# A scheduling planner inside a kernel: new instruction costs, a new price for accumulating DMAs, and two requests moved to other stages

## Chip, cores and metric

The kernel runs on one core of one Trainium2 chip. The metric is the device time of one execution in microseconds (us), inputs and outputs in the chip's memory.

## The reference

Three blocks follow each other. The tensor that passes between them has 2304 rows (4 batches of 576 positions) of 512 columns.

- Attention with a bias: 4 x 8 heads, 576 positions, head size 64, causal, with scores lowered by running sums of a third input.
- A first expert block with one expert: `h = x @ w_in` (512 to 2048), `g = h * sigmoid(1.702 h)`, `g @ w_out`.
- A second expert block with eight experts, all of them used for every row:

```python
logits = x @ w_gate
P = exp(logits - logits.max())
for _ in range(8):                 # rows, then columns, are normalised
    P /= P.sum(1, keepdims=True) + 1e-09
    P /= P.sum(0, keepdims=True) + 1e-09
    P *= N / E
for e in range(8):                 # w1: 512 x 1024, w2: 1024 x 512
    h = np.maximum(x @ w1[e], 0.0)
    out += P[:, e:e + 1] * (h @ w2[e])
```

## The kernel before, in words

The program is written out by Python into five instruction queues (PE, ACT, DVE, POOL, and SP for DMAs), and each queue runs strictly in its written order. A recording layer, the class `Sequencer`, decides that order while the program is built. Every operation on ACT, DVE, POOL and SP is first held back; PE's are issued at once, in the order that the planner takes them. The planner keeps a clock for each engine: `cost` (L127) says how long an operation keeps its engine, `depend` (L187) when a result can be used by another operation (the end of the first plus an entry of `LATENCY`), `issue` (L194) moves the clocks on. `run` lets each engine take, among its held operations that are ready by its clock, the one of lowest `rank`. PE's next step is chosen from the step that is ready first by the same clocks. So all waits are real, but which instruction stands ahead of which on a queue rests on the planner's estimates.

For a DMA the planner keeps one common clock, `dma`: each transfer adds its bytes at 360 bytes per nanosecond and ends 440 ns later, plus `late`, a supplement (2000 ns for background work in the second block). A DMA of background rank is held back while that clock is more than `BACKLOG` (3000 ns) ahead.

`fine` is switched on where the second expert block is prepared (L1824); there other cost formulas hold. For `fine`, a DVE operation keeps its engine 150 ns plus its elements at 0.96 or 1.92 per ns, an ACT operation 165 ns (input in PSUM) or 200 ns plus its elements at 1.2 per ns, with 190 ns more where it also writes a sum.

The second block takes the tokens in three groups `tp` of 768. Both matrix products use a seven-product scheme (Strassen's) on half-size blocks, each number as a pair of f16 parts. For each expert `e` and group `tp` there are four units `unit1` (`x @ w1`; seven products of 6 matmuls of 384 columns) and three units `unit2` (`h @ w2`; seven products M1 to M7 of 12 matmuls of 256 columns). Two units are in flight, each on four PSUM banks A to D. A product is added onto the bank of an earlier one: bank B begins as an ACT copy of A (`B<-A`), C as an ACT copy of B (`C<-B`), and the matmuls that add to a copied bank must wait for the copy. Results of `unit2` are scaled into tiles `y` (4 buffers) by ACT or DVE. For the first expert `y` is written to memory, for the second it is joined with that, and for experts 2 to 6 it is added to `acc_d` in memory by an accumulating DMA from POOL's queue (`leave`), 18 for each expert, 90 in all.

While expert `e` runs, the weights of `e + 1` are prepared in the background, at rank 2: `weight_scales` (L1232) loads all of w1 and w2 in 16 pieces of 256 KB (tiles `wm`, in a ring of 7 buffers that it shares with the loads `wr`) and squares each on ACT to find the largest value; `prep_w1` and `prep_w2` (L1423, L1461) load the weights again (`wr`), form the seven combinations and split them into f16 parts, `w1o` in place and `wo` by way of memory (`w2_d`); `load_w2` (L1483) fetches the latter (`w2o`). `load_x2` fetches a token group (`xt`). `after1` (L2096) and `after2` (L2113) are called when a unit is over, and ask for these. What is asked for then waits in the queues above until the planner finds room.

## Time and profile before

| | |
|---|---|
| median of 3 runs | 2025.22 us |
| the runs | 2023.23 to 2025.8 us |
| span of the profiled execution, first to last instruction | 2019.1 us |
| PE / DVE / ACT / POOL busy | 97% / 69% / 62% / 17% of the span |
| first matmul of the second expert block | near 656 us |
| last matmul | 2013.2 us |

The profile is of one execution; of its own time the page gives the span alone. The median of the runs is 6.1 us longer than that span: what lies around the span, and the spread of the runs. "Idle before" an instruction is how long its engine stood still ahead of it, and the arrow names what ended that. A row of the timeline can stand for several equal instructions that follow each other (x12).

### The profile page before, as it was taken

What the parts mean: (1) busy time and instruction counts of PE and PEld (TensorE: products, weight loads), DVE (VectorE), ACT (ScalarE), POOL (GpSimd) and SP (SyncE); (2) the same over time, 40 slices, a digit from 0 to 9 for tenths busy, and PEclk for the clock granted to TensorE, in tenths of its full rate; (3) what the DMA queues carried; (4) which work ended last, traced back from release to release, by engine and by line L of the source; (5) the groups of instructions that cost most, each with busy time, mean ns of one, the idle gap of its engine ahead of it and who ended that gap; (6) DMA issues with size and microseconds to landing.
All of it is one profiled execution on the core that took longest, in us unless ns stands there. A gap on an engine that the chain in (4) does not pass through costs nothing.

```text
span 2019.1 us, 41044 instructions
## 1 busy us (share of the span) xinstructions
PE 1961.6 (97%) x15683; PEld 1575.5 (78%) x15683; DVE 1398.8 (69%) x3036; ACT 1258.0 (62%) x2571; POOL 335.4 (17%) x376
## 2 busy tenths in 40 slices
PE   6989999999999999999999999999998999999998
PEld 5889999999988777777777777777776777777776
DVE  5886777776643677868857866775775787577555
ACT  4776766766534676666666765756665676566444
POOL 3564444453200000000010100111110000111000
PEclk9999999999999999999999999999999999999999
DMA  7555444453354654566585676667657567666331
GB/s 219 157 175 189 134 134 133 141 145 106 85 139 137 184 171 160 184 199 211 174 216 160 160 228 125 172 175 168 187 148 197 133 177 202 120 187 170 118 129 53
DMA packets 234421, 323.18 MB, mean 160 GB/s; under 512 B 40800, under 2 KB 160288, under 8 KB 234224
## 3 DMA queue, kind: packets, MB, share of 16 engines
q1 hardware_dynamic: 221264, 296.96, 46.5%
q0 software_dynamic: 12960, 23.60, 9.2%
q8 instruction: 123, 2.02, 0.4%
q14 instruction: 74, 0.61, 0.1%
HBM read 231.90 MB, written 84.35 MB: 157 GB/s over the span
## 4 chain that ended last, share of the span: by engine, by line
PE 75%; DVE 9%; DMA 7%; issue 5%; ACT 4%; SPq 0%; POOL 0%; ACTq 0%; DVEq 0%; POOLq 0%
PE C L269 14%; PE D L269 14%; PE A L269 14%; PE hp L269 9%; PE B L269 8%; PE acc L269 5%; PE sp L269 3%; PE op L269 3%; PE tp L269 2%; DMA wm<-in_moe_w_dram 2%; DVE h L269 2%; PE accw L269 2%; DMA w_d<-wo 2%; ACT h L269 1%; DVE t L269 1%
## 5 line engine op out<-in xcount | busy, mean ns | idle before, releaser
L269 PEld LDWEIGHTS <-h 128*128 128x128 f16 x6048 | 592.2, 98 | 111.8 <-issue 32.1
L269 PEld LDWEIGHTS <-w1o 128*128 128x128 f16 x4036 | 394.8, 98 | 252.7 <-issue 1.9
L269 POOL DMA_DIRECT2D acc_d<-y x90 | 77.9, 866 | 1209.4 <-DVE y L269 1117.4
L269 PE MATMUL A<-w2o,h 128*128 128x256 f16 x1728 | 215.0, 273 | 16.0 <-ACT B L269 14.0
L269 PE MATMUL C<-xt,w1o 128*128 128x384 f16 x1152 | 218.6, 326 | 0.2
L269 PE MATMUL D<-xt,w1o 128*128 128x384 f16 x1152 | 216.4, 326 | 0.0
L269 PE MATMUL D<-w2o,h 128*128 128x256 f16 x1728 | 214.8, 273 | 0.3 <-ACT y L269 0.2
L269 PE MATMUL A<-xt,w1o 128*128 128x384 f16 x1152 | 215.0, 326 | 0.1
L269 PE MATMUL C<-w2o,h 128*128 128x256 f16 x1728 | 205.4, 272 | 7.8 <-ACT C L269 6.7
L269 DVE SCALAR_TENSOR_TENSOR h<-hst,h 128x768 f16<-128x768 f32 (+1 forms) x192 | 142.2, 752 | 48.4 <-ACT h L269 47.5
L269 PE MATMUL hp<-xh,wih 128*128 128x256 f32 (+1 forms) x512 | 153.9, 301 | 1.2 <-DVE stats L269 0.6
L269 PE MATMUL hp<-xl,wih 128*128 128x256 f32 (+1 forms) x512 | 151.5, 296 | 0.0
L269 PE MATMUL hp<-xh,wil 128*128 128x256 f32 (+1 forms) x512 | 151.4, 296 | 0.0
L269 ACT ACTIVATE h<-hst 128x768 f16<-128x768 f32 (+1 forms) x192 | 128.9, 678 | 6.1 <-DVE hst L269 6.0
L269 ACT COPY C<-B 128x384 f32<-128x384 f32 (+1 forms) x168 | 71.4, 425 | 85.1 <-PE B L269 68.6
L269 ACT ACTIVATE hst<-A 128x384 f32<-128x384 f32 x96 | 47.0, 490 | 119.2 <-PE A L269 118.5
L269 ACT ACTIVATE sm<-sm,stats 64x576 f32<-64x576 f32 (+4 forms) x160 | 94.6, 600 | 37.0 <-DVE stats L269 36.6
L269 PE MATMUL acc<-gh,woh 128*128 128x256 f32 x384 | 110.9, 289 | 0.0
L269 PE MATMUL B<-w2o,h 128*128 128x256 f16 x864 | 109.7, 275 | 0.0
L269 PE MATMUL B<-xt,w1o 128*128 128x384 f16 x576 | 109.3, 326 | 0.0
L269 PE MATMUL acc<-gl,woh 128*128 128x256 f32 x384 | 108.5, 282 | 0.0
L269 PE MATMUL acc<-gh,wol 128*128 128x256 f32 x384 | 108.4, 282 | 0.0
(235 smaller groups left out, 4041.9 us busy)
## 6 DMA issues: line engine op xcount, KB each, us to landing
xt<-xc_d SPq DMA_DIRECT2D x168, 384.0 KB
wm<-in_moe_w_dram SPq DMA_DIRECT2D x112, 256.0 KB
w2o<-w_d SPq DMA_DIRECT2D x56, 512.0 KB
wr<-in_moe_w_dram SPq DMA_DIRECT2D x112, 256.0 KB
w_d<-wo SPq DMA_DIRECT2D x98, 256.0 KB
acc_d<-y POOLq DMA_DIRECT2D x90, 256.0 KB, 6.0
kq<-in_qk_dram SPq DMA_DIRECT2D x32, 448.0 KB
st<-in_moe_w_in_dram SPq DMA_DIRECT2D x16, 512.0 KB
```

The source lines that it names most:

```text
L269: self.seq.submit(self.name, what, lambda: method(*args, **named), outs, ins)
```

## The change

Cost formulas of the planner, for the second block (`fine`): a DVE operation keeps its engine 66 ns (was 150) plus its elements, and 60 (was 63) for a scalar taken from a tile; an ACT operation 50 or 90 ns (was 165 or 200), 100 (was 95) for such a scalar and 93 (was 190) for a sum. What was taken off comes back as a `tail`: the result counts as written 85 (DVE) or 110 ns (ACT) after the engine is free, 90 more with a sum. A dependent operation on the same engine is ready 34 ns after that (it was the full latency between engines, 128 or 150).

DMAs: an accumulating DMA counts 3.6 times its bytes on the planner's DMA clock. The 16 loads of `weight_scales` count as landing 3000 ns later (`LATE`), for experts 2 and up.

Requests: `weight_scales(e + 1)` is asked for after the first unit1 of group 0 (was: after the fourth), `prep_w2(e + 1)` after the third unit2 of group 0 (was: after the fourth unit1 of group 1).

```diff
--- before.py
+++ after.py
@@ -37,8 +37,11 @@
 ASKED = 12
 BACKLOG = 3000
 N_KF = 4
+ADDING = 3.6
+AFTER_OWN = 34
 N_F = 14
 NEXT_V = 11
+LATE = 3000.0
 
 LATENCY = {
     "PE": 197, "ACT": 150, "DVE": 128, "POOL": 75,
@@ -47,7 +50,7 @@
 
 
 class Op:
-    __slots__ = ("engine", "call", "cost", "ready", "end", "waits", "after", "rank", "number", "nbytes", "late")
+    __slots__ = ("engine", "call", "cost", "ready", "end", "waits", "after", "rank", "number", "nbytes", "late", "tail")
 
 
 class Sequencer:
@@ -124,7 +127,7 @@
             n *= x
         return n
 
-    def cost(self, engine, what, out, ins):
+    def cost(self, engine, what, out, ins, sums=False):
         n = max(self.size(x) for x in [out] + ins[:2])
         psum = any(x.space == PSUM for x in ins)
         if self.fine:
@@ -133,9 +136,9 @@
             by = any(self.size(x) == 1 for x in ins[1:]) and n > 1
             if engine == "DVE":
                 quick = what in ("tensor_copy", "tensor_scalar") and not psum
-                return 150 + 63 * by + n / (1.92 if quick else 0.96)
+                return 66 + 60 * by + n / (1.92 if quick else 0.96)
             if engine == "ACT":
-                return (165 if psum else 200) + 95 * by + n / 1.2
+                return (50 if psum else 90) + 100 * by + 93 * sums + n / 1.2
         if engine == "PE":
             n = self.size(out)
             if what == "transpose":
@@ -150,17 +153,22 @@
         return 80 + n * {"memset": 0.3, "tensor_scalar": 2.7}.get(what, 2.24)
 
 
-    def submit(self, engine, what, call, outs, ins):
+    def submit(self, engine, what, call, outs, ins, adds=False):
         op = Op()
         op.engine, op.call, op.end, op.rank, op.number = engine, call, None, self.rank, self.count
-        op.ready, op.waits, op.after, op.nbytes = 0.0, set(), [], 0
+        op.ready, op.waits, op.after, op.nbytes, op.tail = 0.0, set(), [], 0, 0
         op.late = self.late + (2000 if self.fine and self.rank else 0)
         self.count += 1
         if what == "dma_start":
             op.cost = 60 if engine == "SP" else 1000
             op.nbytes = self.size(outs[0]) * outs[0].shape[0] * (2 if self.fine and outs[0].dtype == F16 else 4)
+            if adds and self.fine:
+                op.nbytes *= ADDING
         else:
-            op.cost = self.cost(engine, what, outs[0], ins) + (190 if len(outs) > 1 else 0)
+            sums = len(outs) > 1
+            op.cost = self.cost(engine, what, outs[0], ins, sums) + (190 if sums and not self.fine else 0)
+            if self.fine:
+                op.tail = {"DVE": 85, "ACT": 110}.get(engine, 0) + 90 * sums
         for ap, writes in [(x, False) for x in ins] + [(x, True) for x in outs]:
             name = ap.tensor.name
             if name in self.outside:
@@ -183,11 +191,12 @@
         else:
             self.held[engine].append(op)
 
-    @staticmethod
-    def depend(op, on):
+    def depend(self, op, on):
         if on.end is None:
             op.waits.add(on)
             on.after.append(op)
+        elif self.fine and on.engine == op.engine != "PE" and not on.nbytes:
+            op.ready = max(op.ready, on.end + AFTER_OWN)
         elif on.engine != "PE" or op.engine != "PE":
             op.ready = max(op.ready, on.end + LATENCY.get((on.engine, op.engine), LATENCY.get(on.engine, 0)))
 
@@ -197,7 +206,8 @@
                 self.issue(x)
         e = op.engine
         start = max(self.free[e], op.ready)
-        self.free[e] = op.end = start + op.cost
+        self.free[e] = start + op.cost
+        op.end = start + op.cost + op.tail
         if op.nbytes:
             self.issued = max(self.issued, start) + 475
             self.dma = max(self.dma, self.issued + 1200) + op.nbytes / 360
@@ -266,7 +276,7 @@
                 ins = ([lhs] if lhs is not None else []) + aps + list(keys.values())
             else:
                 ins = aps + list(keys.values())
-            self.seq.submit(self.name, what, lambda: method(*args, **named), outs, ins)
+            self.seq.submit(self.name, what, lambda: method(*args, **named), outs, ins, "accum_op" in named)
 
         return ask
 
@@ -1234,15 +1244,19 @@
         mx = mem["small"].tile([128, 2, 8], F32, tag="wmx", name="wmx", bufs=2)
         for i in range(8):
             st = raw([128, 2, 256], "wm")
+            seq.late = LATE if e > 1 else 0.0
             nc.sync.dma_start(
                 out=st, in_=w1[e, i // 4 * 256:i // 4 * 256 + 256, i % 4 * 256:i % 4 * 256 + 256]
                 .rearrange("(c p) f -> p c f", p=128)
             )
+            seq.late = 0.0
             squares(mx[:, 0, i:i + 1], st)
         scale_of(("w1", e), mx[:, 0], True)
         for i in range(8):
             st = raw([128, 1, DM], "wm")
+            seq.late = LATE if e > 1 else 0.0
             nc.sync.dma_start(out=st, in_=w2[e, i * 128:(i + 1) * 128, :].rearrange("p (o d) -> p o d", o=1))
+            seq.late = 0.0
             squares(mx[:, 1, i:i + 1], st)
         scale_of(("w2", e), mx[:, 1], True)
         iw = mem["small"].tile([128, 1], F32, name=f"iw{e}")
@@ -2096,14 +2110,12 @@
     def after1(e, tp, j):
         if j % 2 and tp == NTP - 1 and e + 1 < E:
             later(2, prep_w1, e + 1, j // 2)
+        if (tp, j) == (0, 0) and 0 < e < E - 1:
+            later(2, weight_scales, e + 1)
         if j < NJ - 1:
             return
         if (e, tp) != (E - 1, NTP - 1):
             later(1, load_x2, (tp + 1) % NTP)
-        if tp == 0 and 0 < e < E - 1:
-            later(2, weight_scales, e + 1)
-        if tp == 1 and 0 < e < E - 1:
-            later(2, prep_w2, e + 1)
 
     def after_gate(tp):
         if tp == NTP - 1:
@@ -2111,6 +2123,8 @@
             side.append((x, next(x)))
 
     def after2(e, tp, i):
+        if (tp, i) == (0, 2) and 0 < e < E - 1:
+            later(2, prep_w2, e + 1)
         if (tp, i) == (NTP - 1, 2) and e + 1 < E:
             later(1, load_w2, e + 1)
 
```

No instruction that computes is added or taken away; the queues are in another order. The number of rows on PE is the same (26536), and its first difference stands in the first unit of the second block. Three places, as the built programs have them:

ACT, expert 5, the time of the last unit2 pair of group 0. `wm` is a square of `weight_scales`, B and C are copies into banks, `y` results. Before:

```order
L269 COPY C_20551<-B_20444 128x256
L269 ACTIVATE wm,wmx<-wm 128x512 x2
L269 COPY C_20565<-B_20450 128x256
L269 ACTIVATE wm,wmx<-wm 128x512 x6
L269 ACTIVATE y<-C_20565,pq 128x256
L269 ACTIVATE wm,wmx<-wm 128x512
L269 COPY B_20649<-A_20636 128x256
L269 COPY B_20677<-A_20670 128x384
L269 ACTIVATE y<-D_20652,pq 128x256
L269 ACTIVATE y<-A_20636,pq 128x256
```

Now:

```order
L279 ACTIVATE wm,wmx<-wm 128x512
L279 COPY C_20597<-B_20440 128x256
L279 ACTIVATE wm,wmx<-wm 128x512
L279 COPY B_20613<-A_20600 128x256
L279 ACTIVATE wm,wmx<-wm 128x512 x6
L279 COPY C_20692<-B_20613 128x256
L279 ACTIVATE y<-B_20613,pq 128x256
L279 COPY B_20701<-A_20694 128x384
L279 ACTIVATE wm,wmx<-wm 128x512
L279 ACTIVATE m_20739<-D_20731 128x384
L279 ACTIVATE y<-A_20600,pq 128x256
L279 ACTIVATE y<-C_20692,pq 128x256
```

The six squares in one piece stood ahead of a `y` and a seventh square, and of the copy of A into B for the last unit2 of the group. Now the one square ahead of this copy is the ninth, the six come behind it, and the sixteenth square stands two copies later.

SP, the same expert, the loads between those of `w2o` and those of the second token group. `mx` is a column of maxima, written when eight squares are done. Before:

```order
L269 DMA wm<-in_moe_w_dram 128x2x256 x7
L269 DMA xt<-xc_d_206 128x1536 x7
L269 DMA wm<-in_moe_w_dram 128x2x256
L269 DMA wm<-in_moe_w_dram 128x512 x7
L269 DMA mx_20374<-m_20370 128x1
L269 DMA wm<-in_moe_w_dram 128x512
L269 DMA mx_20387<-m_20383 128x1
L269 DMA row<-mx_20374 128x128
```

Now:

```order
L279 DMA wm<-in_moe_w_dram 128x2x256 x8
L279 DMA xt<-xc_d_206 128x1536 x7
L279 DMA wm<-in_moe_w_dram 128x512 x3
L279 DMA mx_20139<-m_20135 128x1
L279 DMA wm<-in_moe_w_dram 128x512 x5
L279 DMA row<-mx_20139 128x128
L279 DMA mx_20152<-m_20148 128x1
L279 DMA wr<-in_moe_w_dram 128x2x256 x6
L279 DMA row<-mx_20152 128x128
```

The first `mx` now goes out after the eleventh load, behind it five loads; it went out after the fifteenth. One load more stands ahead of `xt`, and the first `wr` loads of `prep_w2` stand ahead of the last `row`.

PE, expert 4, group 2: the end of M6 of one unit2 in bank B and what follows. Before:

```order
L269 MATMUL C1_19863<-w2o_18065,h_19705 128x256
L269 LDWEIGHTS h_19705
L269 MATMUL B0_19771<-w2o_18065,h_19705 128x256
L269 LDWEIGHTS h_19705
L269 MATMUL B0_19771<-w2o_18065,h_19705 128x256
L269 LDWEIGHTS h_19705
L269 MATMUL B0_19771<-w2o_18065,h_19705 128x256
L269 LDWEIGHTS h_19472
L269 MATMUL C0_19898<-w2o_18065,h_19472 128x256
```

Now:

```order
L279 MATMUL B0_19749<-w2o_18066,h_19644 128x256
L279 LDWEIGHTS h_19710
L279 MATMUL B0_19749<-w2o_18066,h_19710 128x256
L279 LDWEIGHTS h_19710
L279 MATMUL B0_19749<-w2o_18066,h_19710 128x256
L279 LDWEIGHTS h_19710
L279 MATMUL B0_19749<-w2o_18066,h_19710 128x256
L279 LDWEIGHTS h_19470
L279 MATMUL C1_19871<-w2o_18066,h_19470 128x256
```

Before, M5 of the same unit, on bank C0, which is the copy of B0, followed at once. Now 12 matmuls of the other unit (C1) stand between M6 and M5.

## Rows read from the trace of the kernel before

**Rows 1.** The page, section 1: busy time, share and instructions of each engine.
```profile
PE 1961.6 (97%) x15683; PEld 1575.5 (78%) x15683; DVE 1398.8 (69%) x3036; ACT 1258.0 (62%) x2571; POOL 335.4 (17%) x376
```

**Rows 2.** Waits of PE over the span: waiting, awaited, total us, times, longest us.
```profile
PE A L269 <- ACT B L269: 14.0, 18, 5.1
...
PE C L269 <- ACT C L269: 6.7, 14, 1.0
```

**Rows 3.** Timeline of PE, second block: start us, us, instruction, [idle before it, releaser].
```profile
691.18 1.47 PE L269 MATMUL A<-w2o,h 128*128 128x256 f16 x12 [0.25 <-ACT B L269]
...
1048.05 1.47 PE L269 MATMUL A<-w2o,h 128*128 128x256 f16 x12 [0.99 <-ACT B L269]
...
1153.22 4.09 PE L269 MATMUL C<-w2o,h 128*128 128x256 f16 x36 [0.50 <-ACT C L269]
...
1216.83 1.47 PE L269 MATMUL A<-w2o,h 128*128 128x256 f16 x12 [0.84 <-ACT B L269]
...
1385.42 1.47 PE L269 MATMUL A<-w2o,h 128*128 128x256 f16 x12 [1.77 <-ACT B L269]
...
1729.28 0.92 PE L269 MATMUL A<-w2o,h 128*128 128x256 f16 x7 [1.70 <-ACT B L269]
...
1878.78 1.47 PE L269 MATMUL A<-w2o,h 128*128 128x256 f16 x12 [0.28 <-ACT B L269]
```

**Rows 4.** Timeline of PE after the longest stop, and in undisturbed work near the end.
```profile
1558.30 2.72 PE L269 MATMUL A<-w2o,h 128*128 128x256 f16 x12 [5.08 <-ACT B L269]
...
1560.81 2.77 PE L269 MATMUL B<-w2o,h 128*128 128x256 f16 x12
...
1563.37 1.56 PE L269 MATMUL D<-w2o,h 128*128 128x256 f16 x12
...
2006.05 1.47 PE L269 MATMUL A<-w2o,h 128*128 128x256 f16 x12
...
2007.36 1.47 PE L269 MATMUL D<-w2o,h 128*128 128x256 f16 x12
```

**Rows 5.** Timeline of ACT around the longest stop.
```profile
1546.65 0.61 ACT L269 ACTIVATE wm<-wm 128x512 f32<-128x512 f32 x1
...
1547.29 0.63 ACT L269 ACTIVATE wm<-wm 128x512 f32<-128x512 f32 x1
...
1554.33 0.63 ACT L269 ACTIVATE wm<-wm 128x512 f32<-128x512 f32 x1 [6.32 <-DMA wm<-in_moe_w_dram]
...
1557.26 0.63 ACT L269 ACTIVATE wm<-wm 128x512 f32<-128x512 f32 x1 [1.24 <-DMA wm<-in_moe_w_dram]
...
1557.88 0.74 ACT L269 COPY B<-A 128x256 f32<-128x256 f32 x2
```

**Rows 6.** Timelines of SP's queue and of POOL, the same time.
```profile
1531.24 3.21 SPq L269 DMA_DIRECT2D xt<-xc_d  x7
...
1539.56 0.33 SPq L269 DMA_DIRECT2D wm<-in_moe_w_dram  x1
1542.22 0.33 SPq L269 DMA_DIRECT2D wm<-in_moe_w_dram  x1
...
1545.72 0.38 SPq L269 DMA_DIRECT2D wm<-in_moe_w_dram  x1
...
1545.73 0.86 POOL L269 DMA_DIRECT2D acc_d<-y  x1 [37.99 <-DVE y L269]
```

**Rows 7.** Windows: stretch, busy PE, PEld, DVE, ACT, POOL (x instructions), PEclk, DMA share, GB/s.
```profile
1535.00:1540.00 5.00, 5.00 (x47) 4.48 (x47) 4.77 (x9) 4.87 (x12) 0.00 (x0) 1.00 0.99 362
1545.00:1550.00 5.00, 4.46 (x41) 4.01 (x41) 1.40 (x3) 3.01 (x11) 2.59 (x3) 1.00 1.08 105
...
1555.00:1560.00 5.00, 1.70 (x9) 1.20 (x9) 0.16 (x1) 2.79 (x9) 0.86 (x1) 0.67 1.01 171
```

**Rows 8.** The accumulating DMAs (tile acc_d): time to landing.
```profile
DMA to landing us min/median/max: 3.9/6.0/15.9
```

**Rows 9.** Groups: line, engine, operation, shapes, count | busy us, mean ns | idle before.
```profile
L269 PE MATMUL C<-xt,w1o 128*128 128x384 f16 x1152 | 218.6, 326 | 0.2
```

## The prediction

> **What bounds the kernel now.** I read the page first, then the waits of PE, then PE's timeline stop by stop, and beside the longest stop the timelines of ACT, SP and POOL. PE is busy for 1961.6 us, 97% of the span [rows 1], so only the time in which it stands still, or runs slowly, can be won; none of its matmuls goes. Then the waits of PE: what is long in the second block are waits for ACT's copies of one bank into another, 14.0 us in 18 stops for `B<-A`, 6.7 us in 14 for `C<-B`, 20.7 us together [rows 2]. PE's timeline, read in windows of 10 us from 650 us to the end, has each of them.
>
> Among the 18, five are long: 0.99, 0.84, 1.77 and 1.70 us [rows 3] and 5.08 us [rows 4], 10.38 us together, one in each of the experts 2 to 6, the five whose results are added by accumulating DMAs. The other 13 are of one kind, 0.25 to 0.28 us, 3.6 us together, the first at 691.18, the last at 1878.78 [rows 3]. Of the 14, five are 0.50 us, the first at 1153.22 [rows 3].
>
> The longest stop tells what the long ones are. ACT had six squares, the 10th to the 15th, in its queue ahead of the copy that PE wanted. The 13th began at 1547.29; then ACT stood still for 6.32 us, until the 14th load had landed, and again 1.24 us for the 16th; at 1557.88 came the copy [rows 5]. I measure from the moment when SP sends the first load of the next tokens, 1531.24: loads 13, 14 and 16 went out 8.3, 11.0 and 14.5 us after it, the last in the same moment as the first accumulating DMA [rows 6]. The 13th had landed before 16.1 us, the 14th landed at 23.1, the 16th at 26.0, 12.1 and 11.5 us behind their issue. In the stretch with plain loads the DMA engines moved 362 GB/s at a share of 0.99; with accumulating ones 105 GB/s at 1.08 [rows 7]. So a byte that is added costs them 362 / 105 x 1.08 / 0.99 = 3.8 times a plain one. The planner knew a factor of 1.
>
> **The change part by part.** *Long stops.* In the new order of expert 5 the copy that was late stands ahead of the six squares, and their loads go out sooner. Counted in PE's order from the same moment, with 1.31 us for twelve matmuls of `unit2` (2006.05 to 2007.36 [rows 4]) and 0.98 for six of `unit1`, which stream three quarters of the columns: the first `mx` can go out 63 matmuls, a `y` and a reduction later, 7.8 us, and loads 12 to 15 behind it, at 0.4 each, from 8.2 to 9.7. That is where the 13th stood before, which was not held up. The first accumulating DMA comes at 11.5 us, earlier than before. The six squares begin at 16.7 and need 0.64 us each (1546.65 to 1547.29 [rows 5]); the copy behind them is wanted by PE at 24.9, later than the 14th load landed before. The 16th load goes out at 16 us, among the accumulating DMAs, and lands at 27.5 if it takes 11.5 again; its square now stands behind one more copy, and the next thing that PE needs of ACT is wanted at 29.5. Expert 3 has the same order. Counted in the same way, experts 2, 4 and 6 have their last loads out by 8 to 10 us, and the accumulating DMAs from 12. I take the five stops as gone: **-10.4**. Bounds: 0 and -10.4.
>
> *The slow clock.* Behind the stop of 5.08 us PE's twelves were 2.51 us (1558.30 to 1560.81) and 2.56 us apart, where 1.31 is usual [rows 4]; the granted clock was 0.67 on average in that stretch [rows 7], the lower of its two levels (1.2 GHz) for part of it, after PE had stood for those 5.08 us. That is 1.20 + 1.25 = 2.45 us. It goes with the stop: **-2.4**, or 0.
>
> *Short stops.* They come from PE's order: too little work between the product that is copied and the one that needs the copy. The order before has 20 copies `B<-A` of `unit2` with only three matmuls between (0.33 us), the order now 5; `C<-B` with nothing between fell from 6 to 2, of which the last stands at the very end in both. With the prices of [rows 3]: 13 stops of 0.28 shrink to a quarter, -2.7, and four of 0.50 go, -2.0. Together **-4.7**; bounds 0 and -9.3, if all of both kinds went except the 1.0 us at the end.
>
> *New stops by tighter planning.* The planner now packs ACT and DVE closer. The pitch of squares of 0.64 us [rows 5] bears the new table out: 90 + 427 + 93 = 610 ns for one, where the old one had 817. What could be lost is slack. In `unit1` the copies `C<-B` with just six matmuls (0.98 us) between are 58, before 17. Those 17 cost at most 0.2 us in all [rows 9], so the nearest row says 0. If each of the 41 new ones came late by the pitch of one square, 0.64 us, that would be 26 us: the other bound. I take **+1.5**, since a few will meet a late DMA.
>
> *Moved requests.* `weight_scales` asks for 16 loads and 16 squares, four writes and reads of maxima; `prep_w2` for 8 loads and 14 writes of 256 KB. All stay, one queue is passed differently: SP has one more `wm` load ahead of `xt`, and a `row`, which waits for its `mx` to land, ahead of the next `xt`. Cover: a token group is needed three units of 84 matmuls (27 us) after the queue gets to it, and the weights a whole expert later. I cost it at nothing; without that cover a late `xt` would stop PE by the landing of a caught load, some 10 us. No stop waits for these loads now, so there is nothing to win either.
>
> *The first part.* Up to the second block PE's order is unchanged, a few ACT and DVE instructions change places behind matmuls: 0.
>
> Sum: -10.4 - 2.4 - 4.7 + 1.5 = **-16.0 us**, from 2019.1 to 2003.1 in the profiled execution, and on the median of the runs, 6.1 us above that span, **2009.2 us**.
>
> One page speaks against this. Here two loads that were out beside accumulating DMAs took 12.1 and 11.5 us [rows 5, 6], as if they stood behind them. The Trainium skill (DMA: Bandwidth & Descriptors, section Queues, rings and completion order) says that each DMA engine takes turns between the queues it has work for, packet by packet. By that rule a load on SP's queue should be held up by POOL's no longer than about its own length, the long stops would not be owed to the added bytes, and the sum would keep the short stops alone, -4.7 + 1.5 = -3.2. The row decides, but it is one place, so the case is a rival.
>
> **The rivals.**
>
> *A part of the long stops stays.* For it: one load of 16 still goes out among the accumulating DMAs in experts 3 and 5, these start earlier than before, and one of them took up to 15.9 us to land [rows 8]. Against it: the slack counted above, which is 1 to 2 us at its least. If each of the five keeps a stop like the mean of the four lesser ones, 1.3 us, 6.6 us come back: 2015.8 us.
>
> *The price of the added bytes is not the cause.* Loads are late for another reason, and the stops move elsewhere at the same size: 2025.2 - 3.2 = 2022.0 us, no difference. That the change does nothing at all is excluded by the orders.
>
> *Slower: results wait for their buffers.* A `y` of the third `unit2` of a group takes the buffer of the first unit's, whose accumulating DMA must have landed. In the first group of these experts the new order gives nearly all results to DVE, so a late landing holds up DVE, behind it the reading of bank D, and so PE. By the order of expert 5 this `y` stands seven twelves (9.2 us) behind the DMA, and PE needs the bank 3.6 us later: it decides where a landing takes over 12.8 us. The median is 6.0 and the longest 15.9 us [rows 8]; no long stop of PE comes from such a buffer now. If each of the five experts got one stop of the worst kind, 5.08 us and 2.45 of slow clock, that would be 37.7 us in place of 12.8, less 3.2: 2025.2 + 24.9 - 3.2 = 2046.9 us.
>
> **How the numbers follow.** Forecast, 0.58: 2009 us, its own range 2004 to 2014 by the bounds of the short stops. Part of the long stops stays, 0.21: 2016. Not the cause, 0.12: 2022. Slower, 0.09: up to 2047, less where fewer experts are hit. A measurement of this kernel can tell about 0.2% from no change, 4 us: faster is below 2021.2, slower above 2029.3. That gives faster 0.79, same 0.12, slower 0.09. The range from 2002 to 2021 leaves out the slower case and most of the third, and a little below.
>
> **What would show it.** Right: no stop of PE over 0.7 us for a copy `B<-A` in experts 2 to 6, ACT's waits for `wm` loads there down to a few us, no stretch of the second block with a clock like 0.67; `B<-A` waits near 1 us in all, `C<-B` below 4; PE's stops some 8 us together. The first part of the order wrong: long stops at the same places with loads 12 to 15 among the accumulating DMAs. The second wrong: short stops as many as before. It would be wrong altogether if stops appear that wait for `y` on DVE, for `xt`, or for `C<-B` in `unit1`.

## The result and the profile after

The changed kernel took **2006.89 us** (median of 4 runs, 2005.06 to 2008.63), the kernel before 2024.22 beside it (2022.15 to 2025.8): a ratio of **0.992**, 95% interval 0.9906 to 0.9934. The forecast was 2009.2. The profiled execution has a span of 2005.0 us, 14.1 less than before, and took 2006.7.

Section 1 of the page of the changed kernel answers to [rows 1]:

```profile
PE 1958.0 (98%) x15683; PEld 1576.3 (79%) x15683; DVE 1395.7 (70%) x3035; ACT 1253.2 (63%) x2572; POOL 335.2 (17%) x376
```

Its waits of PE (waiting, awaited, total us, times, longest us) answer to [rows 2]:

```profile
PE C L279 <- DVE y L279: 6.3, 6, 4.7
PE C L279 <- DVE hst L279: 2.7, 3, 1.5
PE A L279 <- ACT B L279: 2.2, 5, 0.6
...
PE C L279 <- ACT C L279: 1.9, 3, 1.0
...
PE D L279 <- ACT y L279: 1.4, 1, 1.4
```

The waits for bank copies went from 20.7 us to 4.1, and all five long ones of experts 2 to 6 are gone. In their place stand waits for results, 10.4 us. Over the second block PE's timeline has 20 stops of 15.56 us in all, where it had 37 of 23.51. Three of the new ones are long. PE's timeline (start, us, instruction, [idle before it, releaser]), after [rows 3, 4]:

```profile
879.62 2.71 PE L279 MATMUL C<-w2o,h 128*128 128x256 f16 x12 [4.71 <-DVE y L279]
882.14 1.57 PE L279 MATMUL D<-w2o,h 128*128 128x256 f16 x12
883.54 1.47 PE L279 MATMUL A<-w2o,h 128*128 128x256 f16 x12
...
1388.83 1.36 PE L279 MATMUL D<-w2o,h 128*128 128x256 f16 x11 [1.38 <-ACT y L279]
...
1578.37 1.14 PE L279 MATMUL C<-xt,w1o 128*128 128x384 f16 x6 [1.52 <-DVE hst L279]
```

The stop of 4.71 us, in expert 1, brought the slow clock with it: 2.52 us from one twelve to the next, then 1.40, where 1.31 is usual [rows 4]. The granted clock (PEclk, third number from the end) was 0.50 there, the lower of its two levels, 1.2 GHz. The window, and DVE's timeline, which tells what PE waited for:

```profile
879.00:882.00 3.00, 2.38 (x12) 1.65 (x12) 1.30 (x4) 0.00 (x0) 0.00 (x0) 0.50 0.66 180
```

```profile
871.03 0.48 DVE L279 SCALAR_TENSOR_TENSOR y<-D,pq,y 128x256 f32<-128x256 f32 x1 [0.83 <-PE D L279]
878.42 0.75 DVE L279 SCALAR_TENSOR_TENSOR y<-yb,prob,y 128x512 f32<-128x512 f32 x1 [6.91 <-DMA yb<-y_d]
879.09 0.48 DVE L279 SCALAR_TENSOR_TENSOR y<-C,pq,y 128x256 f32<-128x256 f32 x1
```

The planner put an addition of `yb` (expert 0's result, loaded back) ahead of the result that frees bank C, and the addition could begin only 12.2 us after the load's issue (866.25).

One line did not turn out as the forecast had it. ACT's waits, changed kernel, then before:

```profile
ACT wm L279 <- DMA wm<-in_moe_w_dram: 28.5, 20, 8.3
```

```profile
ACT wm L269 <- DMA wm<-in_moe_w_dram: 30.9, 14, 6.3
```

ACT waits for the loads of `wm` nearly as long as it did. ACT's timeline of the changed kernel, beside [rows 5], tells why PE no longer minds:

```profile
1545.20 0.36 ACT L279 COPY C<-B 128x256 f32<-128x256 f32 x1 [7.44 <-DVE y L279]
...
1546.09 0.38 ACT L279 COPY B<-A 128x256 f32<-128x256 f32 x1
...
1550.26 0.63 ACT L279 ACTIVATE wm<-wm 128x512 f32<-128x512 f32 x1 [1.11 <-DMA wm<-in_moe_w_dram]
...
1555.50 0.63 ACT L279 ACTIVATE wm<-wm 128x512 f32<-128x512 f32 x1 [1.53 <-DMA wm<-in_moe_w_dram]
```

The copy that PE wants now stands ahead of the squares that wait. So two questions are left: which part of the change did this, and why the loads are late at all.

### The profile page after: what moved, and what is told of

It reads as the page before. It is cut to its first block, busy times and chain, and to the rows that moved or that the text cites. A ratio compares the mean times of both kernels' runs of the same rounds, so it can differ in the third digit from the quotient of the medians.

```text
span 2005.0 us, 41027 instructions
## 1 busy us (share of the span) xinstructions
PE 1958.0 (98%) x15683; PEld 1576.3 (79%) x15683; DVE 1395.7 (70%) x3035; ACT 1253.2 (63%) x2572; POOL 335.2 (17%) x376
## 4 chain that ended last, share of the span: by engine, by line
PE 74%; DVE 12%; DMA 7%; issue 4%; ACT 3%; SPq 0%; POOL 0%; DVEq 0%; ACTq 0%; POOLq 0%
PE C L279 15%; PE D L279 14%; PE A L279 14%; PE hp L279 8%; PE B L279 7%; PE acc L279 5%; DVE h L279 3%; PE sp L279 3%; PE op L279 3%; PE tp L279 2%; PE accw L279 2%; DMA wm<-in_moe_w_dram 1%; DVE t L279 1%; DMA wr<-in_moe_w_dram 1%; DVE sb L279 1%
## 5 line engine op out<-in xcount | busy, mean ns | idle before, releaser
L279 PE MATMUL C<-w2o,h 128*128 128x256 f16 x1728 | 209.6, 273 | 8.3 <-DVE y L279 6.3
L279 PEld LDWEIGHTS hp<-xh,wih 128*128 128x128 f32 x512 | 97.9, 191 | 4.6 <-PE sp L279 0.9
```

Of the source, the lines that this page charges most:

```text
L279: self.seq.submit(self.name, what, lambda: method(*args, **named), outs, ins, "accum_op" in named)
```

## The experiments

The kernel before had medians of 2024.4 to 2028.3 us in the sets below, so kernels are compared by their ratio to it.

### Are the added bytes why the loads are late?

The kernel before, with

```diff
-                nc.gpsimd.dma_start(out=acc_d[t], in_=y, accum_op=ALU.add)
+                nc.gpsimd.dma_start(out=acc_d[t], in_=y)
```

> The kernel before, in its own order, except that the 90 accumulating DMAs of experts 2 to 6 only write their tile to memory and add nothing (the sum over these experts is left out). Theory (the bytes that are added hold the loads up): the five long stops of PE for B<-A in experts 2 to 6 shrink to under 0.5 us each, the slow clock behind the one at expert 5 goes, ACT's waits for wm loads in these experts fall from some 20 us to a few, and the short stops of 0.28 and 0.50 us stay as they are; the time falls by 10 to 14 us, to 2010 to 2014. Rival (each DMA engine takes turns between the queues, so the loads wait for something else): long stops as before, the time within 4 us of the kernel before.

Measured: 2022.0 us, ratio 0.998 (0.9964 to 0.9997). Waits of PE and of ACT in this kernel:

```profile
PE A L269 <- ACT B L269: 14.9, 19, 3.2
```

```profile
ACT wm L269 <- DMA wm<-in_moe_w_dram: 31.1, 14, 5.2
```

The sum over the experts is left out here, so nothing is added any more; ACT still waits as long for the loads, and the long stops are as many: 1.50, 1.64, 1.12, 3.21 and 3.03 us, 10.5 together. My theory of the loads fell here.

### The three parts alone

Each is the kernel before with one part of the diff. First the durations, tails and the 34 ns:

```diff
+                return 66 + 60 * by + n / (1.92 if quick else 0.96)
+                return (50 if psum else 90) + 100 * by + 93 * sums + n / 1.2
...
+                op.tail = {"DVE": 85, "ACT": 110}.get(engine, 0) + 90 * sums
...
+            op.ready = max(op.ready, on.end + AFTER_OWN)
```

> The kernel before with the new instruction costs, tails and the 34 ns alone: accumulating DMAs count their plain bytes, no supplement for the loads, requests where they were. Its order has no B<-A copy with three matmuls between (20 before) and one C<-B with nothing between (6). Theory (short stops come from the costs, long ones from the price of the added bytes): the 0.28 and 0.50 us stops go, a stop costs about 0.16 us more than its idle row shows, so 4 to 10 us are won; long stops stay in experts 2 to 6: 2014 to 2021. Rival (the costs alone do nearly all): 2010 or less, with no stop over 0.8 us in experts 2 to 6.

Measured: 2044.6 us, ratio 1.0094 (1.0068 to 1.012). The short stops went, and eleven of 2 to 4.3 us came (a text below says twelve), ten of them in experts 2 to 6. The first in expert 2, on PE's timeline and on ACT's:

```profile
1054.77 2.72 PE L279 MATMUL D<-w2o,h 128*128 128x256 f16 x12 [3.16 <-ACT y L279]
```

```profile
1054.25 0.47 ACT L279 ACTIVATE y<-D,pq 128x256 f32<-128x256 f32 x1 [5.49 <-DMA acc_d<-y]
```

The result cannot be written: its buffer is still being read by an accumulating DMA. That is the mechanism of my slower rival.

The price alone:

```diff
+ADDING = 3.6
+LATE = 3000.0
...
```

> The kernel before with the price of 3.6 for added bytes and the 3000 ns supplement alone; old costs, requests where they were. Its order keeps 19 B<-A copies with three matmuls between. Theory: the five long stops go and the slow clock with them, the short ones stay: 10 to 13 us won, 2011 to 2015. Rival (the price does nothing by itself, since squares asked for late still crowd the end of the group): within 4 us of the kernel before, long stops in two or more of the experts 2 to 6.

Measured: 2011.5 us, ratio 0.9933 (0.9907 to 0.9959). The long stops of copies went, down to two of 1.02 and one of 1.92 us.

The moved requests alone:

```diff
+        if (tp, j) == (0, 0) and 0 < e < E - 1:
+            later(2, weight_scales, e + 1)
...
+        if (tp, i) == (0, 2) and 0 < e < E - 1:
+            later(2, prep_w2, e + 1)
...
```

> The kernel before with weight_scales and prep_w2 asked for earlier and nothing else. Theory (a request only enters the queue of held work; the planner's clocks decide where it stands): long and short stops stay, within 5 us of the kernel before. Rival (earlier requests alone bring the loads out ahead of the accumulating DMAs): long stops of experts 2 to 6 under 0.5 us each, 10 us or more won, 2014 or less.

Measured: 2036.8 us, ratio 1.006 (1.0041 to 1.0079). New long stops, the longest 6.47 us at 1232.27 for a `y` on ACT, which had stood 9.48 us for an accumulating DMA.

So the parts don't add up: 0.9933 for the price, 1.0094 and 1.006 for the others, and 0.992 for all. The intervals of the price alone and of all three overlap, so the time does not tell what the other two add to the price.

### The two halves of the price

The kernel before with only the supplement on the loads:

```diff
+LATE = 3000.0
...
```

> The kernel before with one number of the change: the planner takes every load of the second MoE's weight pieces (experts 2 to 7) to land 3 us later. The factor on the accumulating DMAs, the durations and the places of the requests are those of before. Price alone (this number and the factor 3.6) gave 2011.5 us. Theory (the 3 us are what puts the squares behind the copies): the five B<-A stops of over 0.7 us in experts 2 to 6 go, and the time is 2010 to 2015 us. Rival (the factor on the bytes does it, since it is the accumulating DMAs that the planner then sees in the transfers' way): the five stops stay with 8 us or more in all, and the time is 2020 to 2024 us.

Measured: ratio 0.9944 (0.9929 to 0.9959). One long wait for `B<-A` is left (1.52 us, expert 5); but waits for `y` of 1.0 to 1.9 us came in experts 2, 3, 5 and 6, which the whole price did not have.

With only the factor:

```diff
+ADDING = 3.6
...
```

> The other half of the price: the kernel before with the accumulating DMAs counted at 3.6 times their bytes by the planner, and nothing else of the change. Theory (the 3 us on the loads do the work): some of the five long B<-A stops stay, at least 4 us in all, and the time is 2016 to 2024 us. Rival (the factor does it): they go, and the time is 2010 to 2014 us. If both halves give 2012 us, either is enough to push the squares back, and the two numbers are one remedy given twice.

Measured: ratio 0.9997 (0.9987 to 1.0007), with long stops for `B<-A` in all five experts, 15.5 us in all. The 3 us on the loads put the squares behind the copies. The factor does nothing alone; with the 3 us it goes with results that no longer wait for buffers, but 0.9944 and 0.9933 can't be told apart.

### What the tight durations ran into

The kernel with durations alone, and plain stores:

```diff
-                nc.gpsimd.dma_start(out=acc_d[t], in_=y, accum_op=ALU.add)
+                nc.gpsimd.dma_start(out=acc_d[t], in_=y)
```

> The new durations, tails and 34 ns alone (2044.6 us when run), with the results of experts 1 to 6 stored by plain DMAs on POOL's queue in place of accumulating ones; the order of every instruction is that of the run with durations alone, and the output lacks the sum over the experts. In that run twelve stops of 2 to 4.3 us were new, ten of them in experts 2 to 6 where PE waits for a result y (D<-ACT y, C<-DVE y) that itself waits for a y buffer, 5.5 us behind an accumulating DMA at the first of them. Theory (the accumulating DMAs hold the y buffers): the ten stops fall below 1 us each, and the time is 2018 to 2026 us. Rival (the buffers come late because POOL issues the store late, or the tight order does it whatever the store): at least 15 us of the stops stay, and the time is 2035 to 2045 us.

Measured: ratio 0.993 (0.9914 to 0.9947), from 1.0094. Of the ten stops four are left, 2.46, 1.22, 1.80 and 0.91 us. The accumulating DMAs, with a median landing of 6.6 us where the plain stores have 3.7, had held the buffers.

### The whole without one part

The changed kernel with the requests where they were:

```diff
-        if (tp, j) == (0, 0) and 0 < e < E - 1:
-            later(2, weight_scales, e + 1)
...
-        if (tp, i) == (0, 2) and 0 < e < E - 1:
-            later(2, prep_w2, e + 1)
...
```

> The changed kernel with the requests for weight scales and the second weight in their old places: new durations and price without the moves. Price alone gave a ratio of 0.9933, durations alone 1.0094, moves alone 1.006, all three 0.992. Theory (once the planner knows what the DMAs cost, the tighter durations no longer end in waits, and the moved requests cost about the 4.71 us stop at expert 1, where they put thirteen pieces ahead of x and yb, and give little): the stop at 879 us is gone and the time is 2000 to 2006 us, a ratio of 0.988 to 0.991. Rival (the moves are needed, since tighter durations without them make the squares collide with the results): long stops of DVE y or ACT y, 2010 to 2020 us, 0.993 to 0.998.

Measured: ratio 0.9912 (0.9884 to 0.994), the same as the whole within its interval. One stop stands out, 7.43 us at 904.61 in expert 1; without it the block has 8.2 us of stops. DVE had stood 9.36 us for a `yb`, whose load SP had sent right behind an `mx`. (The row names a store; but of the transfers that this instruction waits for, the load's last completion signal, at 898.27, is the one just ahead of its start.) That load took 10.1 us. Of the five ahead of it, the two sent 1.3 and 3.3 us behind the `mx` of 866.26 took 9.2 and 10.3, the others 3.8 to 4.6. SP's queue, then DVE:

```profile
887.80 0.32 SPq L279 DMA_DIRECT2D mx<-m  x1
888.18 0.42 SPq L279 DMA_DIRECT2D yb<-y_d  x1
```

```profile
898.36 0.75 DVE L279 SCALAR_TENSOR_TENSOR y<-yb,prob,y 128x512 f32<-128x512 f32 x1 [9.36 <-DMA acc_d<-y]
```

The changed kernel with the old durations:

```diff
-                return 66 + 60 * by + n / (1.92 if quick else 0.96)
+                return 150 + 63 * by + n / (1.92 if quick else 0.96)
-                return (50 if psum else 90) + 100 * by + 93 * sums + n / 1.2
+                return (165 if psum else 200) + 95 * by + n / 1.2
...
```

> The changed kernel with the old durations: price and moves alone. Theory (durations set the short stops, the price the long ones): the short B<-A stops with three matmuls between come back, some 20 of them at about 0.4 us and 0.16 us more each than their rows show, 10 us in all less what the new stops of the change cost; the time is 2008 to 2016 us, a ratio of 0.992 to 0.996, with 35 stops or so. Rival (the moves do harm without the durations too, as alone, 1.006): 2020 to 2036 us.

Measured: ratio 1.0079 (1.0049 to 1.0109): the rival. Five stops of 2.7 to 5.6 us for `C<-B` or `hst` in `unit1`; before the last of them DVE had waited 7.80 us for a weight load, the fourth of the six below, which landed 14.4 us behind its issue, and again an `mx` stands just ahead of them. SP's queue and DVE:

```profile
1744.95 0.33 SPq L275 DMA_DIRECT2D mx<-m  x1
1745.37 4.03 SPq L275 DMA_DIRECT2D wr<-in_moe_w_dram  x6
```

```profile
1761.44 0.69 DVE L275 TENSOR_TENSOR wt<-wr 128x512 f32<-128x512 f32 x1 [7.80 <-DMA wr<-in_moe_w_dram]
```

### Two attempts at the stop in expert 1

```diff
+                seq.late = 5000.0 if e == 1 else 0.0
                 nc.sync.dma_start(out=before[t], in_=(y0_d if e == 1 else acc_d)[t])
+                seq.late = 0.0
```

> The changed kernel with one more supplement: the planner takes the loads of y0 for expert 1's results (the tiles yb) to land 5 us later, as it does 3 us for the weight pieces. Theory (the 4.71 us stop of PE at 879.62 us and the slow clock after it, 1.21 and 1.40 us, come from an addition of yb that the planner put on DVE ahead of a result that PE's bank waits for): the stop goes, no granted clock below 0.95 is left from 870 to 890 us, and the time is 1998 to 2003 us. Rival (the transfers are simply late there, and the wait turns up at the next bank, y buffer or at hst): 2004 to 2009 us, with stops of 3 us or more in all between 860 and 960 us.

Measured: ratio 0.9914 (0.9899 to 0.9929), no better than the changed kernel. The stop went, and three of 2.72, 2.41 and 1.46 us came within 30 us, the first for a `y` that waited for its buffer; one of 3.07 us came in expert 6.

```diff
-                nc.sync.dma_start(out=before[t], in_=(y0_d if e == 1 else acc_d)[t])
+                if e == 1:
+                    nc.gpsimd.dma_start(out=before[t], in_=y0_d[t])
+                else:
+                    nc.sync.dma_start(out=before[t], in_=acc_d[t])
```

> The changed kernel with the loads of y0 for expert 1's results (yb) asked for on POOL's queue in place of SP's, where they stand behind sixteen weight pieces and seven x tiles (issue at 866.25 us, addition at 878.42 us, 12 us). POOL issues nothing else in expert 1. The planner's order on DVE and ACT stays nearly the same: the addition still stands ahead of the result that PE's bank C waits for. Theory (the loads are late because they stand in SP's queue behind 5.9 MB of others; each DMA engine takes turns between queues, as the Trainium skill's page on DMA: Bandwidth & Descriptors has it under Queues, rings and completion order): yb lands within 6 us of its issue, the 4.71 us stop at 879.62 us falls below 1 us and the clock stays at 1.00 there: 2000 to 2003 us, a ratio to before of 0.988 to 0.990. Rival (the transfers of that stretch are slow on every queue): yb still takes 10 us or more, and the stop stays, 2005 to 2009 us.

Measured: ratio 0.9907 (0.9883 to 0.9931). The stop fell to 0.78 us, but others grew (2.52 and 2.71 us in experts 3 and 5), so no gain can be told. The loads are what matters. SP's queue, POOL and DVE:

```profile
879.69 0.32 SPq L279 DMA_DIRECT2D mx<-m  x1
```

```profile
875.64 0.54 POOL L279 DMA_DIRECT2D yb<-y_d  x1 [2.08 <-DMA wm<-in_moe_w_dram]
880.75 0.54 POOL L279 DMA_DIRECT2D yb<-y_d  x1 [4.57 <-DVE y L279]
882.07 0.54 POOL L279 DMA_DIRECT2D yb<-y_d  x1 [0.79 <-DVE y L279]
```

```profile
881.02 0.75 DVE L279 SCALAR_TENSOR_TENSOR y<-yb,prob,y 128x512 f32<-128x512 f32 x1 [0.57 <-DMA yb<-y_d]
891.18 0.75 DVE L279 SCALAR_TENSOR_TENSOR y<-yb,prob,y 128x512 f32<-128x512 f32 x1 [5.34 <-DMA yb<-y_d]
894.07 0.75 DVE L279 SCALAR_TENSOR_TENSOR y<-yb,prob,y 128x512 f32<-128x512 f32 x1 [0.95 <-DMA yb<-y_d]
```

The load of 875.64 could be used 5.4 us later; those of 880.75 and 882.07, issued behind the `mx` but on another queue, took 10.4 and 12.0. Their own queue did not save them.

### The 4-byte writes

So I looked at what follows an `mx<-m` in the kernel before. `scale_of` sends 128 partial maxima, one float in each partition, to DRAM: 128 packets of 4 bytes. Two of these, on SP's queue:

```profile
870.76 0.33 SPq L269 DMA_DIRECT2D mx<-m  x1
...
1545.29 0.33 SPq L269 DMA_DIRECT2D mx<-m  x1
```

Windows of 2.5 us (stretch, busy engines, PEclk, DMA share, GB/s) around the first, in expert 1, where nothing accumulates:

```profile
867.50:870.00 2.50, 2.50 (x26) 2.24 (x24) 1.78 (x5) 2.12 (x6) 0.00 (x0) 1.00 1.03 401
870.00:872.50 2.50, 2.50 (x25) 2.22 (x23) 1.69 (x5) 1.03 (x3) 0.00 (x0) 1.00 1.06 398
872.50:875.00 2.50, 1.86 (x18) 1.55 (x16) 0.94 (x3) 2.45 (x9) 0.00 (x0) 1.00 1.23 368
875.00:877.50 2.50, 2.50 (x25) 2.24 (x24) 0.75 (x2) 1.91 (x7) 0.00 (x0) 1.00 1.22 83
```

and around the second, at the longest stop:

```profile
1542.50:1545.00 2.50, 2.41 (x23) 2.01 (x21) 1.18 (x4) 1.38 (x4) 0.00 (x0) 1.00 0.97 367
1545.00:1547.50 2.50, 1.96 (x19) 1.76 (x19) 0.89 (x2) 2.50 (x10) 0.86 (x1) 1.00 0.73 153
1547.50:1550.00 2.50, 2.50 (x25) 2.25 (x23) 0.51 (x2) 0.51 (x2) 1.73 (x2) 1.00 1.43 57
```

The share comes to 1.22 and 1.43 while the rate falls to 83 and 57, so packets take longer. The trace's packet records, put together by stretch of that place (SP's queue; larger ones are packets of 1 KB and more). Each load has 16 packets of 4 bytes of its own, so the second column is not the `mx` alone; its 128 lie between 1546.5 and 1547.2:

```
stretch, us         4-byte packets   larger ones: count, mean ns, longest ns
1543.5 to 1545.5          42              264     86     96
1545.5 to 1546.5           1              103    145    626
1546.5 to 1548.5         162              116    420   4328
1548.5 to 1550.5           2               14    727   5886
```

The 4-byte packets take 9 ns each by their records; those behind them up to 5.9 us. Fifteen larger ones of 0.4 to 0.6 us stand up to a microsecond ahead of them; all over 1 us come behind. The accumulating ones are caught as well: 23 of them from 1550.5 to 1552.5 with a mean of 1.1 us, and 191 from 1556.5 to 1558.5 with 0.19. Of the 459 packets of 1 KB and more that took over 1 us from 630 us on, 321 begin within 12 us behind the issue of one of the 14 `mx`, an eighth of that time. Of those on SP's and POOL's queues, 160 took over 2 us, and all 160 begin there.

The last experiment is the changed kernel with the maxima turned before they leave:

```diff
-        nc.sync.dma_start(out=d.rearrange("o p -> p o"), in_=m)
...
+        nc.vector.tensor_copy(wide, m.to_broadcast([128, 32]))
+        nc.vector.transpose(turned, wide)
+        nc.sync.dma_start(out=d.rearrange("o (k c) -> (o k) c", c=32), in_=turned[0:128:32, :])
```

> The changed kernel with one transfer in another form. For each weight's scale the 128 partial maxima (m, one float in each partition) go to DRAM by a DMA of 128 packets of 4 bytes (mx<-m); here DVE copies them to 32 columns and turns the blocks of 32 by 32, so that the same 512 bytes leave as four packets of 128 bytes. Reason: in every trace so far the DMA rate falls from some 390 GB/s to below 160 within 5 us of an mx<-m that meets other transfers: in the kernel before at 1545.29 us (366 GB/s five us ahead of it, 37 at a share of 1.36 in the third to fifth us after it), in expert 1 without an accumulating DMA as well (870.76 us), and with plain stores. Theory (the 4-byte writes to DRAM stall the engines' other packets, so weight pieces, yb and the accumulating DMAs all land late): the rate after mx<-m stays above 250 GB/s while loads are outstanding, yb at expert 1 lands within 8 us, the stops of 4.71, 1.38 and 1.52 us go with the slow clock after the first, 11 us in all, and the time is 1994 to 2000 us on the chip that gave 2024 for the kernel before, a ratio of 0.985 to 0.988. Rival 1 (four packets stall as 128 do, or the crowd of transfers ends just there): the rate still falls below 160 GB/s, and the ratio stays at 0.990 to 0.993. Rival 2 (the loads come sooner, but the new order's stops move elsewhere, as with yb on another queue): the rate stays up, and the ratio is 0.988 to 0.992.

Measured: 1996.17 us (1995.05 to 1998.61), ratio **0.9847** (0.9828 to 0.9865). It beats both kernels, the changed one by 0.9847 / 0.992 = 0.993, by their ratios to the kernel before. Its page, waits of PE and of ACT:

```profile
PE 1954.5 (98%) x15683; PEld 1576.1 (79%) x15683; DVE 1396.2 (70%) x3059; ACT 1253.9 (63%) x2580; POOL 334.8 (17%) x376
```

```profile
PE A L279 <- ACT B L279: 2.6, 6, 0.5
...
PE C L279 <- ACT C L279: 1.9, 3, 1.0
...
PE C L279 <- DVE y L279: 1.6, 5, 0.6
```

```profile
ACT wm L279 <- DMA wm<-in_moe_w_dram: 1.8, 4, 0.6
```

The second block has 15 stops of 6.91 us in all, none over 1 us, and the clock is 0.999. ACT's waits for `wm` fell from 28.5 us to 1.8. In expert 5 the `mx` goes out at 1529.53, four loads behind it:

```profile
1529.53 0.54 SPq L279 DMA_DIRECT2D mx<-turned  x1
```

```profile
1529.50:1532.00 2.50, 2.50 (x25) 2.25 (x23) 1.43 (x4) 0.36 (x1) 0.00 (x0) 1.00 1.04 388
1532.00:1534.50 2.50, 2.50 (x25) 2.25 (x23) 0.97 (x2) 0.00 (x0) 0.00 (x0) 1.00 1.03 370
1534.50:1537.00 2.50, 2.50 (x25) 2.24 (x24) 0.97 (x2) 1.38 (x4) 0.86 (x1) 1.00 0.86 188
1537.00:1539.50 2.50, 2.50 (x25) 2.24 (x24) 0.48 (x1) 1.35 (x6) 1.72 (x2) 1.00 0.81 92
```

The first two windows keep their rate. The third, at 188 GB/s, is below the 250 of the theory, but it holds the last packets of the loads and the first accumulating ones, and none of those of the loads took over 0.12 us; the fourth has accumulating DMAs alone. The four loads landed 4.4 to 5.5 us after their issue, where the five behind the first `mx` of expert 5 took 9.1 to 9.5 in the changed kernel.

The two small operations on DVE also shift the planner's order, so not every part of the time need be the packets'. For the packets themselves the records are plain: from 630 us on, 221 of 1 KB and more on SP's and POOL's queues took over 2 us in the changed kernel, all but one within 12 us behind an `mx`; here none did, the longest took 1.9.

The longest landing of an accumulating DMA fell too, from 14.5 us to 8.7. Time to landing, changed kernel, then this one:

```profile
DMA to landing us min/median/max: 3.8/5.6/14.5
```

```profile
DMA to landing us min/median/max: 3.8/4.6/8.7
```

## Why the prediction was right, and where it was not

*Long stops, -10.4.* The size held: 10.38 us of stops went, because the copies now stand ahead of the late squares, as worked out for expert 5. The cause of the lateness did not hold. The step that failed is "so a byte that is added costs them 3.8 times a plain one" as the reason of the late loads: with plain stores ACT waited for them as long. What held them up was the `mx` that SP sent at 1545.29, 0.4 us ahead of the 16th load. I had left that row out; it stands between those of [rows 6]. The window from which I took the 3.8, 1545 to 1550 [rows 7], was misread too: by the packet records 8 of its 252 packets of 2 KB are accumulating ones, and the others, plain packets of SP's queue, have 0.94 of its share of 1.08. An added byte does cost more, but less than that: a packet of 2 KB takes 178 ns in the median of the last kernel where a plain one takes 84, a factor of 2.1. (The last window above gives 3.3 against the first, 92 GB/s at 0.81 to 388 at 1.04; it holds packets that took up to 0.93 us.) My estimate that loads 12 to 15 would come in time was not borne out: they went out 0.3 to 2.1 us later than counted, and landed 9.1 to 9.5 us later, where the 13th had taken 7.6; the order gets along with it.

*The slow clock, -2.4.* It went, and came back behind the new stop of 4.71 us: 1.21 + 0.09 us by the spacing of the twelves. Net -1.15.

*Short stops, -4.7.* Mis-sized. Waits for copies fell from 20.7 to 4.1 us; less the five long ones that is 6.2, not 4.7. A stop also costs more than its row shows: twelve matmuls are shown as 1.47 us, but undisturbed twelves start 1.31 apart [rows 4], since their ends are modelled, so 0.16 us are hidden at each stop. With 17 stops fewer that is another 2.7 us, by estimate; the start-to-start times at the stops give 0.16 us each as well.

*New stops, +1.5.* Mis-sized the other way: 10.4 us of waits for results, of which 0.8 were there before, and the clock. The place was one that I had not costed: in expert 1, a `yb` load.

*The sum.* Stops shown -7.95, hidden part -2.7, clock -1.15: -11.8 of the span's -14.1. Of the rest 0.65 lies ahead of the second block, whose first stop ends at 656.24 us in place of 656.89, and some 2 us are stops too short for the views, under 0.15 us: 10 of 0.56 us in place of 16 of 1.63, each with its hidden part. That accounts for the span to within 0.4 us. Errors of both signs met at -16.0 and 2009.2, and that they nearly cancelled is luck. By its own signs the prediction did less well: the waits for `wm` stayed, PE's stops are 15.56 us and not 8, a stretch with the slow clock is there, and stops for `y` on DVE, which it named as a sign of being wrong altogether, came (6.3 us). One of 4.71 us and its clock were too little to undo the gain.

*Moved requests, 0.* In the whole they are worth nothing that can be told (0.9912 without them). But alone, and with the price under old durations, they cost 0.6% and 1.5% (1.0079 against 0.9933); the rows of that run point to what then stands behind an `mx`.

*The rivals.* "The price of the added bytes is not the cause" was right on the cause and wrong on the outcome, since planning for late loads helps whatever makes them late. The rule of the Trainium skill beside it (DMA: Bandwidth & Descriptors, Queues, rings and completion order), that engines take turns between queues, agrees with the plain stores' result; it does not protect a queue here, as the `yb` loads on POOL's show (10.4 and 12.0 us). The slower rival, results that wait for their buffers, is what the durations alone (1.0094) and the moves alone met. With the price they did not.

Shown is that packets of over 2 us no longer come, and that ACT no longer waits for the loads in the second block, when the 128 packets of 4 bytes are four of 128. Why small writes stall the rest is not. The same page of the Trainium skill, under Specifications, says that below 512 bytes a DMA engine reads, modifies and writes; that holds for four packets of 128 bytes as well, and no packet behind them takes over 1.9 us. Whether size or number decides was not tried, nor was this edit in the kernel before.

## What to carry to other kernels

When loads are late, look at the small transfers that went out just ahead of them before blaming the large ones: a high share of the DMA engines at a low rate is the sign. A column of maxima can be turned before it is stored; the kernel with that was 0.7% faster here. And when a planner gets tighter durations, let it plan for late DMAs in the same step; without that, the slack that went came back here as waits for buffers.

## What the runs showed of the hardware

- A DMA of 128 packets of 4 bytes to DRAM, beside other transfers, was followed by some 10 us in which packets of 2 KB took up to 5.9 us on SP's queue, where 0.09 is usual, and up to 5.5 on POOL's, where 0.18 is (kernel before). The same 512 bytes in four packets did not do this.
- An accumulating packet of 2 KB takes 178 ns in the median, a plain load's 84.
- The DMA share is the time of packets, not work: 57 GB/s at 1.43.
- A stop of PE costs 0.16 us more than its row shows, because the matmuls before it are drawn to a modelled end (1.47 us for twelve that start 1.31 apart).
